# A recurrent-memory attention kernel: another order in its first segment, and output rows in one transfer

## The chip, the cores and the metric

The kernel runs on one core of a Trainium2 chip. The metric is the device time of one execution in microseconds (us), taken as the median of several runs. The engines are named as in the profile: PE (TensorE matmul) and PEld (its weight load), DVE (VectorE), ACT (ScalarE), POOL (GpSimd) and SP (SyncE). SP and POOL issue nearly all DMA transfers here; SP's go to the queue named q1 in the profile, POOL's to q0, and all of them run on the core's 16 DMA engines.

## What is computed

Two branches are mixed by a gate, on 2048 rows of 1024 values in bfloat16:

```python
g = sigmoid((x * gate_w).sum(-1, keepdims=True))
b = (gelu(x @ w_gate) * (x @ w_up)) @ w_down          # 1024 -> 3584 -> 1024
mem = mem0                                            # 8 rows
for s in range(64):                                   # segments of 32 rows
    h = concat([mem, x[32*s : 32*s+32]])              # 40 rows
    q, k, v = h @ Wq, h @ Wk, h @ Wv                  # 32 heads of 128
    p = softmax(where(mask, q @ k.T / sqrt(128), -1e9))
    o = (p @ v) @ Wo                                  # 40 rows of 1024
    mem = o[:8]
    a[32*s : 32*s+32] = o[8:]
out = g * a + (1 - g) * b
```

The mask lets every row see the 8 memory rows, and otherwise is causal. The attention branch is a recurrence: a segment needs the memory that the one before it produced. Its weights (4 x 8 MB) don't fit into SBUF.

## The kernel before

The program is written out by hand, instruction by instruction. A small scheduler (`_Sched`) takes each operation with its engine and the keys that it reads and writes, and puts in the semaphore waits. Each engine runs its operations in the order in which the program emits them, so the order of the `emit_` calls is the order of work on each engine, and POOL's and SP's transfers are issued in that order too. An operation that waits holds up all that stands behind it on its engine.

**Feed-forward branch (0 to about 597 us).** Four blocks of 512 rows: gate and up products, then the down product (L494). The last block's results go through SBUF buffers (`extra`, part of `arena`, `qk` and `oe`) and by 20 transfers on POOL's queue (L518) to DRAM, as `b_scr`. So `qk` can be overwritten only when its transfers have landed. In this time the attention weights begin to be loaded.

**Attention (597 us to the end): 64 segments.** A part of the weights stays in `arena`. The rest is streamed in every segment: 18 loads of 512 KB and one of 256 KB from a packed copy `w_scr` into `ring`, a buffer of 10 slots of 256 KB (L616, on SP). A load is issued when PE has freed its slots (`slot_free`). The main steps of a segment, with the names that the change touches:

- `emit_P(m, h, pos)`: one 1024-long product for m in q, k, v and half h of the heads, in eight pieces over the inner dimension (L948). `KORD` gives the order of the pieces for segments above 0, and `KCS` for segment 0. Pieces 6 and 7 come from the ring; in segment 0, pieces 4 and 5 of q/0 as well.
- In segment 0 each `emit_P` also does a product with `xe` (`emit_ext`, L835), which gives the first 8 rows of 4 segments ahead. Its result is copied to a staging area (`stage`, keys `rx` 0 to 4 in `arena` chunk 20, and `rowsx` for v/1) by ACT (L849). For q and k, PE then transposes it, DVE puts it back in another order (L874, 0.88 us) and POOL stores it as `qk_scr` (L877). The transposes and the rest form a job; `first_go` and `flush` emit the waiting jobs. For v, POOL stores it as `v_scr` (L852).
- `emit_T` (L992, L997, L999): transposes of q or k into `qk`. `emit_qke` (L1006): copies the extra rows from the staging area into `qk`.
- `emit_S(o)`: scores of pair o (L1025) and the softmax: DVE L1032 to L1036, Exp on ACT L1038, DVE L1039 to L1045, the last into `pn`. `emit_PT(o)`: transposes of `pn` (L1055) and a copy by DVE into `ptb` (L1060). `emit_PV(o)`: product with v (L1066) and copies by ACT into `oT` (L1074) and `oe` (L1075).
- `emit_vt` copies v to `vt` on ACT (L985). In segment 0 the extra rows of v come for half 0 by small transfers (`load_vte`, L720), and for half 1 by `emit_sel(par)`: a product with a selection matrix (L1195) and a copy by ACT (L1197).
- `emit_O(o, pos)`: product of the 8 heads of group o with Wo (L1107). In segment 0 `OHS` gives the order of the heads. Wo of heads 24 to 27 (group 3) lies in chunk 20, where the staging area was: `load_o3(k, xs)` (L885, on POOL) loads one of these four blocks over the staging places xs, and so waits for all that reads them.
- `keep`, `back`, `back_all`: pieces 4 and 5 of q/0 are kept in PSUM through the segment by transposes (L895, with a DVE copy at L901), and put back into free buffers at its end.

**The end of a segment.** ACT copies the 8 memory rows out (L1306), PE transposes them (L1317), DVE puts them into `hT` (L1322), and the next segment can start. DVE computes the gated mix into `bo` (L1325), a tile of 128 partitions by 256: partition 32*q + r holds columns 256*q to 256*q + 255 of row r. Four transfers on POOL's queue, one for each q, write it to the output (L1332), each with its own semaphore. Later in the next segment `load_b` loads `bo` again, when they have landed. In every fourth segment four more transfers (L1343) write the first 8 rows of four segments from `pn`, behind those of `bo` on POOL.

Of the kernel before, what the change touches and what calls it, by code (L numbers as in the profile page):

```python
# [128 lines left out]
def bass_gated_mix__memory_aug_recurrent_mem_tr__geglu_ffn__prompt_kernel(  # L129
# [38 lines left out]
    with ExitStack() as es:  # L168
# [367 lines left out]
                dst = chunk(c).rearrange("p (h d) -> p h d", h=4)  # L536
            op("sp", lambda e: e.dma_start(dst, src), w=[A(c)], dsem=f"a{c}")

        KCS = {0: (0, 6, 1, 2, 7, 3, 4, 5), ('k', 1): (6, 7, 0, 1, 2, 3, 4, 5), ('v', 1): (6, 7, 0, 1, 2, 3, 4, 5), ('v', 0): (6, 7, 0, 1, 2, 3, 4, 5), ('q', 1): (6, 7, 0, 1, 2, 3, 4, 5)}
        OHS = (0, 1, 4, 5, 2, 3, 6, 7)  # L540
        KORD = {('q', 0): (5, 6, 2, 1, 7, 3, 4, 0), ('q', 1): (0, 6, 1, 4, 7, 3, 5, 2), ('k', 0): (5, 2, 6, 7, 0, 1, 4, 3), ('k', 1): (0, 2, 3, 6, 7, 5, 4, 1), ('v', 0): (0, 6, 1, 2, 4, 3, 7, 5), ('v', 1): (4, 6, 1, 2, 7, 3, 0, 5)}
        OORD = ((1, 4, 5, 0, 2, 3, 6, 7), (0, 4, 1, 5, 3, 6, 2, 7), (0, 4, 1, 5, 2, 3, 6, 7), (0, 4, 1, 5, 2, 3, 6, 7))
# [185 lines left out]
        def rows_of(s):  # L728
            n = SEG if s + 1 < NSEG else NR
            v = of[s * SEG + EXT:s * SEG + EXT + n, :]  # L730
            return [(v[:, q * 256:(q + 1) * 256], bo[32 * q:32 * q + n, :]) for q in range(4)]
# [66 lines left out]
        for s in range(NSEG):  # L798
# [19 lines left out]
            def flush():  # L818
                while post:
                    go, put = post.pop(0)  # L820
                    put(go())


            def first_go():
                go, put = post.pop(0)
                put(go())
# [57 lines left out]
            def load_o3(k, xs):  # L884
                op("pool", lambda e: e.dma_start(chunk(20)[:, k * 1024:(k + 1) * 1024], A_Wo[24 + k, :, :]),  # L885
                   w=[("A20", k)] + [("rx", x) for x in xs], dsem=("b1", "b2", "b3", "a20")[k])
# [96 lines left out]
            def emit_vt(h, par, s=s):  # L983
                bank = acc(s, ("v", h))
                op("act", lambda e: e.activation(vt[0:2 * SEG, par, :], PB[bank][64 * par:64 * par + 64, :], ACTF.Copy),  # L985
                   r=[P(bank)], w=[("vt", par)])
# [11 lines left out]
                else:  # L998
                    op("dve", lambda e: e.tensor_copy(qk[:, m, :, 0:SEG, :], src), r=[P(B_T)], w=[("qk", m)])  # L999

            def emit_qke(h, s=s):
                if s == 0:
                    for mi, m in enumerate("qk"):
                        rx, kx, _ = stage(m, h)
                        src = rx[:, 0:128].rearrange("p (g x) -> p g x", g=4)
                        op("dve", lambda e, mi=mi, src=src: e.tensor_copy(  # L1006
                            qk[:, mi, :, SEG:L, :].rearrange("p g c i -> p g (c i)"), src), r=kx, w=[("qke",)])
                    if h == 1:
                        load_ext(1, 0)
                    return  # L1010
                op("dve", lambda e: e.tensor_copy(qk[:, :, :, SEG:L, :].rearrange("p m g c i -> p m g (c i)"), qkst[:, :, :, :]),
                   r=[("qkst",)], w=[("qke",)])
                if h == 1 and s + 1 < NSEG:
                    load_ext(s + 1, 0)
                elif h == 0:
                    load_ext(s, 1)
# [81 lines left out]

            def emit_O(o, pos, s=s, B_O=B_O):
                for x in pos:  # L1100
                    k = OORD[o][x] if s else OHS[x]
                    u, keys = unit(s, "o", o, k)

                    def mk(e, u=u, k=k, x=x):
                        ins = None
                        for q in range(4):
                            ins = e.matmul(PB[B_O][32 * q:32 * q + 32, 0:256], lhsT=oT[:, o % 2, k, :],  # L1107
                                           rhs=u[q // 2][:, (q % 2) * 256:(q % 2 + 1) * 256],
                                           start=(o == 0 and x == 0), stop=(o == NO - 1 and x == 7),
                                           skip_group_check=True)  # L1110
                        return ins
                    op("pe", mk, r=[("oT", o % 2)] + keys, w=[P(B_O)])
                    if "o" in jobs:
                        if k >= 4 and ("o", o, k) not in single:
                            do_oe(o, k, u, keys)
                        else:
                            later.append(lambda u=u, keys=keys, k=k: do_oe(o, k, u, keys))
                    slot_free(uses(s, "o", o, k))
# [11 lines left out]
                           r=[("bscr", jobs["o"], y) for y in range(GR)], w=[("rowsx", q)], dsem="be%d" % q)  # L1130

            if s == 0:
                emit_P("q", 0, ALL[:5])
                op("pe", lambda e: e.matmul(PB[B_S][:, 0:320], lhsT=pnz[:, 0:128], rhs=pnz, start=True, stop=True),
                   r=[("init", "pn")], w=[P(B_S)])
                emit_P("q", 0, ALL[5:])
                emit_P("k", 0, ALL[:5])
                emit_T(0)
                emit_P("k", 0, ALL[5:])
                emit_P("q", 1, ALL[:2])  # L1140
                first_go()
                sel = bo[:, 0:4 * EXT]
                op("dve", lambda e, sel=sel: e.tensor_copy(
# [3 lines left out]
                load_o3(3, (6,))  # L1147
                load_single(("o", 3, 4))
                load_single(("o", 3, 5))
                emit_P("q", 1, ALL[2:5])  # L1150
                emit_T(1)
                emit_P("q", 1, ALL[5:])
                emit_P("v", 0, (0,))
                first_go()
                emit_P("v", 0, ALL[1:6])
                first_go()
                emit_P("v", 0, (6, 7))
                emit_qke(0)
                emit_S(0)
                emit_vt(0, 0)  # L1160
                emit_vt(0, 1)
                load_vte(0, 0, 0)
                load_vte(0, 0, 1)
                vput.pop(0)()
                emit_P("k", 1, (0, 1, 2, 3, 4))
                emit_PT(0)
                emit_S(1)
                emit_T(0, "act")
                flush()
                emit_P("k", 1, (5, 6, 7))  # L1170
                emit_P("v", 1, (0, 1, 2))
                emit_T(1)
                emit_PV(0)
                emit_P("v", 1, (3,))
                emit_PT(1)
                emit_P("v", 1, (4,))
                flush()
                emit_qke(1)
                emit_P("v", 1, (5,))
                load_o3(2, (4,))  # L1180
                emit_PV(1)
                emit_P("v", 1, (6,))
                emit_S(2)
                emit_P("v", 1, (7,))
                load_x(1)
                load_o3(0, (0, 1))
                load_o3(1, (2, 3))
                emit_vt(1, 0)
                emit_vt(1, 1)
# [8 lines left out]
                       r=[P(bank)], w=[("vte", par), ("vte", par, 0)])  # L1198

                emit_O(0, ALL)  # L1200
                emit_O(1, LO)
                emit_sel(0)
                emit_O(1, (4, 5, 6))
                emit_PT(2)
                emit_S(3)
                emit_sel(1)
                load_b(0)
                emit_O(1, (7,))
                emit_PV(2)
                back_all("act", ("q", 0, 5, 1))  # L1210
                emit_O(2, ALL)
                emit_PT(3)
                emit_PV(3)
                back_all("dve", ("q", 0, 5, 0))
                emit_O(3, ALL)
# [112 lines left out]
            for put, bank in ends:  # L1328
                put(bank)
            last = s == NSEG - 1  # L1330
            for x, (d, b) in enumerate(rows_of(s)):
                op(("sp", "act")[x % 2] if last else "pool", lambda e, d=d, b=b: e.dma_start(d, b),  # L1332
                   r=[("bo", x)], w=[("out", s, x)], dsem="%s%d" % ("end" if last else "out", x))
            if "o" in jobs:
                j = jobs["o"]
                op("dve", lambda e, j=j: e.scalar_tensor_tensor(
# [52 lines left out]
```

## Time and profile before

| | us |
|---|---|
| median of 3 runs (lowest, highest) | 2498.48 (2494.85, 2501.15) |
| profiled execution, device time | 2490.87 |
| its span, first to last instruction | 2489.0 |
| PE busy | 2256.3 (91%) |
| DVE busy | 1169.8 (47%) |
| ACT busy | 930.9 (37%) |
| POOL busy | 653.4 (26%) |
| end of segment 0 (L1322 begins) | 646.0 |
| mean granted TensorE clock | 0.988 |

A busy PE in this profile is not PE at its peak, since matmuls are pipelined and their ends are modelled. POOL's busy time here is the time of building its DMA transfers. In a line of a group, the part after the bar is busy time and the mean of one instruction in ns, and then the idle time of the engine just before them with what ended it. In the timeline, the brackets hold the idle time before an instruction and what ended it. In a line of waits, the three numbers are the sum in us, how often, and the longest.

### The profile page before, as it was taken

To read this page: it belongs to the slowest core of one execution; us is meant where nothing else is said; L and a number is where in the kernel's file an instruction comes from. 1 tells how busy PE (TensorE), PEld (TensorE's weight loads), DVE (VectorE), ACT (ScalarE), POOL (GpSimd) and SP (SyncE) were. 2 spreads that over 40 slices of the span, in tenths; PEclk is the share of its full clock that TensorE was granted. 3 is DMA by queue.
4 is the path that set the end of the run, shared out by engine and by line. 5 is a ranking of instruction groups with operands and counts; after the bars stand their busy time and mean duration, and the time that the engine had idled before them with its cause. 6 is when DMAs were issued, how large, how long until landed. Compare 5 with 4: busy or idle time off the path is not lost.

```text
span 2489.0 us, 77539 instructions
## 1 busy us (share of the span) xinstructions
PE 2256.3 (91%) x33977; PEld 1112.8 (45%) x33977; DVE 1169.8 (47%) x3435; ACT 930.9 (37%) x2196; POOL 653.4 (26%) x1162
## 2 busy tenths in 40 slices
PE   9999999999889888988988898888889888889887
PEld 4444444444444444444444444444444444444443
DVE  5626264451444444544454544444444444455444
ACT  4314132221334343434443444434444434444433
POOL 1010103102232323233323323332323232323222
PEclk9999999999899999999999999999999999999988
DMA  8727354468999999999999999999999999999997
GB/s 273 257 71 256 97 179 123 144 229 302 322 348 365 365 371 348 373 359 379 375 377 354 374 366 374 352 356 367 375 370 378 365 363 376 362 377 374 371 362 281
DMA packets 328689, 797.10 MB, mean 320 GB/s; under 512 B 52728, under 2 KB 116456, under 8 KB 327584
## 3 DMA queue, kind: packets, MB, share of 16 engines
q1 hardware_dynamic: 284336, 736.78, 81.2%
q0 software_dynamic: 43872, 55.31, 7.1%
q8 instruction: 267, 4.37, 0.7%
q14 instruction: 70, 0.57, 0.1%
q10 hardware_dynamic: 144, 0.06, 0.0%
HBM read 764.52 MB, written 37.22 MB: 322 GB/s over the span
## 4 chain that ended last, share of the span: by engine, by line
PE 58%; DMA 26%; DVE 9%; ACT 4%; issue 3%; POOL 0%; SPq 0%; DVEq 0%; POOLq 0%
DMA ring<-w_scr 25%; PE pba L948 7%; PE pbb L948 7%; PE pbc L835 5%; PE pbb L1107 3%; PE pbe L1055 3%; PE pba L1107 2%; PE pbe L992 2%; PE pba L449 2%; PE pbb L449 2%; PE pbh L449 2%; PE pbg L449 2%; PE pbf L449 2%; PE pbe L449 2%; PE pbd L449 2%
## 5 line engine op out<-in xcount | busy, mean ns | idle before, releaser
L948 PE MATMUL pba<-arena,hT 128*32 128x512 bf16 x4416 | 350.6, 384 | 0.0
L948 PE MATMUL pbb<-arena,hT 128*32 128x512 bf16 x4416 | 342.6, 385 | 0.3 <-issue 0.3
L999 DVE COPY qk<-pbe 128x512 bf16<-128x512 bf16 x129 | 89.2, 692 | 363.3 <-PE pbe L992 358.6
L723 POOL DMA_DIRECT2D vt<-v_scr x252 | 147.9, 591 | 371.6 <-PE pbf L1066 234.1
L1038 ACT ACTIVATE pbd<-pbd 104x160 f32<-104x160 f32 x256 | 71.9, 281 | 432.2 <-DVE pbd L1036 432.2
L1060 DVE COPY ptb<-pbe 80x320 bf16<-80x320 bf16 x256 | 82.1, 321 | 240.5 <-PE pbe L1055 240.5
L1332 POOL DMA_DIRECT2D out_dram<-bo x252 | 125.8, 506 | 246.1 <-DVE bo L1325 244.9
L948 PE MATMUL pba<-ring,hT 128*32 128x512 bf16 x1542 | 153.2, 388 | 28.9 <-DMA ring<-w_scr 27.7
L835 PE MATMUL pbc<-arena,xe 128*32 128x512 bf16 x2208 | 174.4, 380 | 0.7 <-ACT rowsx L849 0.5
L948 PE MATMUL pbb<-ring,hT 128*32 128x512 bf16 x1536 | 151.9, 390 | 25.3 <-DMA ring<-w_scr 23.5
L954 ACT ACTIVATE rows<-pba 128x512 bf16<-128x512 f32 x128 | 76.6, 598 | 234.2 <-PE pba L948 234.2
L948 PEld LDWEIGHTS pba<-arena,hT 128*32 128x32 bf16 x4416 | 111.8, 97 | 97.9 <-issue 5.6
L1045 DVE TENSOR_TENSOR pn<-pbd,rr 104x256 bf16<-104x256 f32 (+1 forms) x512 | 142.3, 319 | 27.7 <-DMA out_dram<-pn 19.4
L948 PEld LDWEIGHTS pbb<-arena,hT 128*32 128x32 bf16 x4416 | 109.7, 97 | 93.0 <-issue 8.0
L954 ACT ACTIVATE rows<-pbb 128x512 bf16<-128x512 f32 x128 | 76.6, 598 | 173.7 <-PE pbb L948 173.6
L877 POOL DMA_DIRECT2D qk_scr<-rowsx x60 | 47.5, 791 | 344.2 <-DVE rowsx L874 281.6
L1107 PE MATMUL pba<-arena,oT 128*32 128x256 bf16 x2176 | 120.9, 281 | 14.1 <-ACT oT L1074 12.5
L1107 PE MATMUL pbb<-arena,oT 128*32 128x256 bf16 x2176 | 121.9, 279 | 12.7 <-ACT oT L1074 10.8
L1055 PE MATMUL pbe<-ident,pn 104*80 104x104 bf16 x1024 | 95.4, 216 | 40.9 <-DVE pn L1045 21.6
L1107 PE MATMUL pba<-ring,oT 128*32 128x256 bf16 x1792 | 107.0, 277 | 20.0 <-DMA ring<-w_scr 19.1
L1039 DVE TENSOR_REDUCE rs<-pbd 104x4 f32<-104x160 f32 x256 | 83.0, 324 | 88.9 <-ACT pbd L1038 88.9
L1107 PE MATMUL pbb<-ring,oT 128*32 128x256 bf16 x1792 | 113.5, 275 | 7.9 <-DMA ring<-w_scr 7.2
(260 smaller groups left out, 4355.2 us busy)
## 6 DMA issues: line engine op xcount, KB each, us to landing
ring<-w_scr SPq DMA_DIRECT2D x973, 512.0 KB, 6.3
ring<-w_scr SPq DMA_DIRECT2D x486, 256.0 KB, 5.9
arena<-in_B_w_gate_dram SPq DMA_DIRECT2D x27, 1024.0 KB, 5.5
arena<-in_B_w_up_dram SPq DMA_DIRECT2D x27, 1024.0 KB, 7.7
qkst<-qk_scr POOLq DMA_DIRECT2D x126, 64.0 KB, 5.2
qk_scr<-rowsx POOLq DMA_DIRECT2D x60, 128.0 KB, 5.6
arena<-in_B_w_down_dram SPq DMA_DIRECT2D x7, 1024.0 KB, 11.9
arena<-in_A_Wk_dram SPq DMA_DIRECT2D x6, 1024.0 KB, 6.9
```

The costliest lines, as they stand in the source:

```text
L449: ins = e.matmul(PB[bank][:, :], lhsT=wv[:, kc, col:col + 128], rhs=xb[:, kc, :], start=(kc == 0), stop=(kc == KC - 1))
L723: op("pool", lambda e: e.dma_start(vt[2 * SEG:KEYS, par, :], v_scr[s // GR, h, 2 * par:2 * par + 2, s % GR, :, :]), r=[("vscr", s // GR, h ...
L835: ins = e.matmul(PB[B_X][32 * gq:32 * gq + 32, :], lhsT=xe[:, us[-1], :], rhs=us[gq // 2][0][gq % 2], start=(n == 0), stop=(n == KC - 1), ...
L948: ins = e.matmul(PB[bank][32 * gq:32 * gq + 32, :], lhsT=hT[:, kc, :], rhs=us[gq // 2][0][gq % 2], start=(x == 0), stop=(x == KC - 1), ski ...
L954: op("act", lambda e: e.activation(rows[:, :], PB[bank][:, :], ACTF.Copy), r=[P(bank)], w=[("rows",)])
L999: op("dve", lambda e: e.tensor_copy(qk[:, m, :, 0:SEG, :], src), r=[P(B_T)], w=[("qk", m)])
L1039: op("dve", lambda e: e.tensor_reduce(rsv, sv, AX.X, ALU.add), r=[P(B_S)], w=[("rs",)])
L1045: op("dve", lambda e, c0=c0, k0=k0, n=n: e.tensor_tensor(out=pn[0:104, :, c0:c0 + 2 * n].rearrange("p i (two c) -> p i two c", two=2), in0 ...
L1055: ins = e.transpose(PBV[B_PT][0:KEYS, 512 + i * 128:512 + i * 128 + 104], pn[0:104, i, :], ident[0:104, 0:104])
L1060: op("dve", lambda e: e.tensor_copy(ptb[0:KEYS, :, :, :], src), r=[P(B_PT)], w=[("ptb",)] + first)
L1107: ins = e.matmul(PB[B_O][32 * q:32 * q + 32, 0:256], lhsT=oT[:, o % 2, k, :], rhs=u[q // 2][:, (q % 2) * 256:(q % 2 + 1) * 256], start=(o ...
L1332: op(("sp", "act")[x % 2] if last else "pool", lambda e, d=d, b=b: e.dma_start(d, b), r=[("bo", x)], w=[("out", s, x)], dsem="%s%d" % ("en ...
```

## The change

Two things are changed. In segment 0 the order of many steps is another one: q/0 takes its pieces in another order, `emit_S(0)` and its copies come ahead of most of v/0, `emit_qke(1)` is split into its q and its k copy, Wo blocks 0 and 2 are loaded earlier, the flush of k/1's job and `emit_PV(0)` change places with pieces of v/1, the selection products stand elsewhere, and group 3 of the output product takes its heads in another order. In all segments but the last, the four output transfers are one, which has the four column blocks as its outer dimension on the DRAM side and all 128 partitions on the SBUF side, with one semaphore.

```diff
-        KCS = {0: (0, 6, 1, 2, 7, 3, 4, 5), ..., ('q', 1): (6, 7, 0, 1, 2, 3, 4, 5)}
+        KCS = {0: (0, 6, 1, 2, 7, 3, 4, 5), ..., ('q', 1): (6, 7, 0, 1, 2, 3, 4, 5), ('q', 0): (0, 6, 7, 4, 5, 1, 2, 3)}
+        OHS3 = (3, 4, 5, 6, 7, 2, 0, 1)
         OHS = (0, 1, 4, 5, 2, 3, 6, 7)
...
-            def emit_qke(h, s=s):
+            def emit_qke(h, s=s, ms=(0, 1)):
                 if s == 0:
-                    for mi, m in enumerate("qk"):
+                    for mi in ms:
+                        m = "qk"[mi]
...
-                    if h == 1:
+                    if h == 1 and ms[-1] == 1:
                         load_ext(1, 0)
...
-                    k = OORD[o][x] if s else OHS[x]
+                    k = OORD[o][x] if s else (OHS, OHS, OHS, OHS3)[o][x]
...
             if s == 0:
-                emit_P("q", 0, ALL[:5])
+                emit_P("q", 0, (0,))
                 op("pe", lambda e: e.matmul(PB[B_S][:, 0:320], lhsT=pnz[:, 0:128], rhs=pnz, start=True, stop=True),
                    r=[("init", "pn")], w=[P(B_S)])
-                emit_P("q", 0, ALL[5:])
+                emit_P("q", 0, (1, 2, 3, 4, 5, 6, 7))
                 emit_P("k", 0, ALL[:5])
                 emit_T(0)
                 emit_P("k", 0, ALL[5:])
-                emit_P("q", 1, ALL[:2])
+                emit_P("q", 1, ALL[:3])
                 first_go()
...
-                emit_P("q", 1, ALL[2:5])
+                emit_P("q", 1, ALL[3:5])
                 emit_T(1)
                 emit_P("q", 1, ALL[5:])
-                emit_P("v", 0, (0,))
                 first_go()
-                emit_P("v", 0, ALL[1:6])
-                first_go()
-                emit_P("v", 0, (6, 7))
+                emit_P("v", 0, (0, 1, 2))
                 emit_qke(0)
                 emit_S(0)
+                emit_P("v", 0, (3, 4))
+                first_go()
+                emit_P("v", 0, (5, 6, 7))
                 emit_vt(0, 0)
                 emit_vt(0, 1)
                 load_vte(0, 0, 0)
                 load_vte(0, 0, 1)
                 vput.pop(0)()
-                emit_P("k", 1, (0, 1, 2, 3, 4))
+                emit_P("k", 1, (0, 1, 2, 3))
                 emit_PT(0)
                 emit_S(1)
+                emit_qke(1, ms=(0,))
+                load_o3(0, (0, 1))
+                load_o3(2, (4,))
                 emit_T(0, "act")
-                flush()
-                emit_P("k", 1, (5, 6, 7))
+                emit_P("k", 1, (4, 5, 6, 7))
                 emit_P("v", 1, (0, 1, 2))
                 emit_T(1)
+                emit_P("v", 1, (3,))
+                flush()
+                emit_P("v", 1, (4,))
                 emit_PV(0)
-                emit_P("v", 1, (3,))
                 emit_PT(1)
-                emit_P("v", 1, (4,))
-                flush()
-                emit_qke(1)
+                emit_qke(1, ms=(1,))
                 emit_P("v", 1, (5,))
-                load_o3(2, (4,))
+                emit_S(2)
                 emit_PV(1)
-                emit_P("v", 1, (6,))
-                emit_S(2)
-                emit_P("v", 1, (7,))
+                emit_P("v", 1, (6, 7))
                 load_x(1)
-                load_o3(0, (0, 1))
                 load_o3(1, (2, 3))
...
                 emit_O(0, ALL)
+                emit_sel(0)
                 emit_O(1, LO)
-                emit_sel(0)
-                emit_O(1, (4, 5, 6))
                 emit_PT(2)
                 emit_S(3)
+                emit_O(1, HI)
+                emit_PV(2)
                 emit_sel(1)
                 load_b(0)
-                emit_O(1, (7,))
-                emit_PV(2)
-                back_all("act", ("q", 0, 5, 1))
                 emit_O(2, ALL)
                 emit_PT(3)
+                back_all("act", ("q", 0, 5, 1))
                 emit_PV(3)
                 back_all("dve", ("q", 0, 5, 0))
                 emit_O(3, ALL)
...
             last = s == NSEG - 1
-            for x, (d, b) in enumerate(rows_of(s)):
-                op(("sp", "act")[x % 2] if last else "pool", lambda e, d=d, b=b: e.dma_start(d, b),
-                   r=[("bo", x)], w=[("out", s, x)], dsem="%s%d" % ("end" if last else "out", x))
+            if last:
+                for x, (d, b) in enumerate(rows_of(s)):
+                    op(("sp", "act")[x % 2], lambda e, d=d, b=b: e.dma_start(d, b),
+                       r=[("bo", x)], w=[("out", s, x)], dsem="end%d" % x)
+            else:
+                op("pool", lambda e, s=s: e.dma_start(
+                    of[s * SEG + EXT:(s + 1) * SEG + EXT, :].rearrange("r (q c) -> q r c", q=4), bo[:, :]),
+                   r=[("bo", x) for x in range(4)], w=[("out", s, x) for x in range(4)], dsem="out0")
```

More of the change, by code (lines that the diff above doesn't have):

```diff
@@ L537, in load_need @@
             op("sp", lambda e: e.dma_start(dst, src), w=[A(c)], dsem=f"a{c}")
-        KCS = {0: (0, 6, 1, 2, 7, 3, 4, 5), ('k', 1): (6, 7, 0, 1, 2, 3, 4, 5), ('v', 1): (6, 7, 0, 1, 2, 3, 4, 5), ('v', 0): (6, 7, 0, 1, 2, 3, 4, 5), ('q', 1): (6, 7, 0, 1, 2, 3, 4, 5)}
+        KCS = {0: (0, 6, 1, 2, 7, 3, 4, 5), ('k', 1): (6, 7, 0, 1, 2, 3, 4, 5), ('v', 1): (6, 7, 0, 1, 2, 3, 4, 5), ('v', 0): (6, 7, 0, 1, 2, 3, 4, 5), ('q', 1): (6, 7, 0, 1, 2, 3, 4, 5), ('q', 0): (0, 6, 7, 4, 5, 1, 2, 3)}
+        OHS3 = (3, 4, 5, 6, 7, 2, 0, 1)
         OHS = (0, 1, 4, 5, 2, 3, 6, 7)
```

## The prediction

> **What bounds the kernel now.** I read the page's slices first, then its queues and its chain, then windows around the first segment and over the rest, then the two places that the change edits: the first segment's instructions in order of time, and POOL's groups. From the page:
>
> ```profile
> PEclk9999999999899999999999999999999999999988
> DMA  8727354468999999999999999999999999999997
> ...
> q1 hardware_dynamic: 284336, 736.78, 81.2%
> q0 software_dynamic: 43872, 55.31, 7.1%
> ...
> PE 58%; DMA 26%; DVE 9%; ACT 4%; issue 3%; POOL 0%; SPq 0%; DVEq 0%; POOLq 0%
> ```
>
> From slice 11 on, the DMA engines are busy without a gap. The chain names weight loads (26%) and PE, no POOL: the ring that SP feeds and the PE that empties it release one another. One engine moves 736.78 MB / (0.812 x 16 x 2489 us) = 22.8 GB/s. Windows of the whole core (us, then PE, PEld, DVE, ACT, POOL busy, PEclk, DMA share, GB/s):
>
> ```profile
> 625.00:630.00 5.00, 4.69 (x80) 2.26 (x76) 2.47 (x9) 2.27 (x6) 0.00 (x0) 1.00 0.56 203
> 630.00:635.00 5.00, 4.74 (x113) 2.91 (x106) 3.54 (x15) 2.79 (x7) 2.91 (x5) 1.00 0.80 243
> 635.00:640.00 5.00, 2.83 (x47) 1.36 (x45) 2.26 (x9) 2.44 (x6) 2.14 (x4) 0.79 0.92 331
> 640.00:645.00 5.00, 2.56 (x38) 1.30 (x36) 1.01 (x2) 0.50 (x2) 0.00 (x0) 0.50 1.03 411
> ...
> 700.00:2389.00 1689.00, 1495.49 (x28292) 757.94 (x28290) 808.27 (x2750) 690.64 (x1659) 521.10 (x917) 1.00 1.00 367
> ```
>
> Segments 1 to 63 are DMA-bound (share 1.00), so an edit there is worth what it changes in DMA work. Segment 0 (597 to 646 us) is not: PE loses 4.6 us in 635 to 645, and DMA loses 3.2 us in 625 to 635. The end of segment 0, in order of time:
>
> ```profile
> 635.89 0.54 POOL L885 DMA_DIRECT2D arena<-in_A_Wo_dram  x1 [1.89 <-DMA qk_scr<-arena]
> ...
> 636.45 0.59 ACT L1197 ACTIVATE vt<-pbb 16x512 bf16<-16x512 f32 x1
> ...
> 637.06 0.38 ACT L1074 ACTIVATE oT<-pbf 128x256 bf16<-128x256 f32 x1
> ...
> 637.50 0.40 PE L1107 MATMUL pba<-arena,oT 128*32 128x256 bf16 x8 [1.82 <-ACT oT L1074]
> ...
> 643.41 0.62 PE L1107 MATMUL pba<-arena,oT 128*32 128x256 bf16 x8 [1.55 <-DMA arena<-in_A_Wo_dram]
> ```
>
> Two stalls stand out: 1.82 us for oT of pair 2, whose copy queues on ACT behind the second selection's copy (0.59), and 1.55 us for a Wo block whose load left POOL at 635.89 and landed 7.5 us later.
>
> **Segment 0, part by part.** (a) q/0 takes pieces 7, 4, 5 earlier and the dummy matmul moves up. The transposes of 4 and 5 now end inside q/0; they cost PE two stalls of 0.46 (604.29, 606.14). I count 0: the chain has b_scr<-qk from 605.45 for 5.27 us, and the first copy into qk (L999) can't begin before it lands (610.85), so PE waits there anyway. Without that cover it would be -0.9.
>
> (b) S(0) moves ahead of v/0's last five pieces. Before, PE lost 0.33 at S(0) and 0.55 at PT(0). After, S(0) follows three pieces (3 x 0.22) behind k/0's transposes, but needs the staging copy (0.88) and two copies (0.42): about 0.9 lost; the softmax (2.7 us) then runs beside v/0, and PT(0) loses nothing. Sum 0, between -0.9 and +1.1.
>
> (c) POOL's queue. q/1's staging store now stands behind that softmax on DVE, so it leaves about 1.5 us later than 620.26, and the four vt<-arena loads (2.1 us) with it; PV(0) is moved back by two pieces and a flush, which hides that; uncovered it costs 1.5. Wo blocks 0 and 2 are issued early, but block 2 overwrites v/0's stage and waits for v_scr, issued near 625 and 5.2 us to landing: POOL stands until 630. Behind it stand k/1's store, qkst, hT and Wo block 1. So k/1's store leaves at about 630.5 (before 631.09), and block 1, which waits for that store (4.5 us), lands about 0.6 earlier, near 642.8. Splitting qke(1) moves two copies of 0.21 and hides in DVE's idle time.
>
> (d) sel(1) after PV(2) takes its 0.59 off ACT ahead of oT: -0.6. S(3)'s Exp stays ahead of oT, so the other 1.2 remain. sel(0) now follows only O(0); it may lose up to 0.4 to ACT.
>
> (e) O(3) in order 3, 4, 5, 6, 7, 2, 0, 1 uses block 1 last. Before, the last 7 heads ran after 643.41 at half clock (to 645.1); after, one runs past 642.8: -1.4, between -1.9 and 0. back_all("act") behind PT(3) has 1.03 us of ACT time while O(2) runs: 0.
>
> Sum -2.0, between -4.7 and +3. It survives, since DMA's idle time in 610 to 660 exceeds it.
>
> **The output transfer, 63 times.** POOL's groups, by form:
>
> ```profile
> L1332 POOL DMA_DIRECT2D out_dram<-bo x244 | 121.8, 506 | 233.7 <-DVE bo L1325 232.5 <-issue 1.2
> ...
> L1343 POOL DMA_DIRECT2D out_dram<-pn x60 | 35.5, 599 | 0.1
> ...
> L737 POOL DMA_DIRECT2D bo<-b_scr x60 | 33.1, 552 | 3.3 <-issue 2.1 <-DMA out_dram<-bo 0.6
> ```
>
> Four issues of 506 ns become one of 552 (128 rows, L737) to 599 (four blocks, L1343): -1.4 us of POOL per segment, off the path (POOL is busy 31%). The wait is the same as before, on one DVE instruction, so nothing new queues behind it.
>
> In DMA work, the trace's packet records after 600 us have POOL's completions as 4 B packets of 9.4 ns: 48 fewer over 16 engines, -28 ns. The old transfers show as 16 packets of 1,024 B (46.6 ns) each. The 16 KB transfers of L1343, four blocks on the DRAM side, show none of that size: they go in 4 packets of 4,096 B (177 ns), with twelve fillers of 32 B (14.3 ns). The new transfer has four blocks too, so I take 16 packets of 4,096 B on four engines: 16 x 177 against 64 x 46.6 is -9 ns per engine, the fillers +11. Sum -26 ns, x 63 = -1.7 us. The other side: four engines get 16 KB where each had 4, 0.72 against 0.18 us, and every ring load waits for its slowest engine: +0.54 us x 63 = +34. I take no loss: by the issues and landings of the ring, three or more loads (1.4 us each at 367 GB/s) are under way 93% of the time, so an engine 0.54 behind doesn't leave the others idle, if the four engines change from segment to segment. That they do is likely: vt<-v_scr has two blocks, and 32 KB per segment always on the same two would hold them 1.4 us of 29, leaving DMA at 0.95, not 1.00.
>
> The page "DMA: Bandwidth & Descriptors" of the Trainium skill (section "Why a DMA increments its semaphore by 16 and not by 1") lets a transfer use the largest k up to 16 that divides the slowest dimension of both sides, and lets GpSimd's transfers rotate over the engines. Its k of 4 here agrees with the four packets above; the rotation no row shows directly. By the section "Rules for kernel authors" of the same page of the Trainium skill, four small transfers should be one large one, which would promise a gain where the k rule threatens a loss.
>
> Every fourth segment, POOL's output rows stand ahead of the four stores of pn; these would leave 1.4 us sooner.
>
> ```profile
> DVE pn L1045 <- DMA out_dram<-pn: 19.4, 13, 2.6
> ```
>
> I take 0: in these segments the transposes that need pn begin 1.3 to 2.7 us after pn is written. The bound is what DMA idles there: by the packets its share is 0.978 of 28.6 us, so 15 x 0.63 = -9.
>
> **Sum.** -2.0 - 1.7 = -3.7 us. The profiled execution took 2490.87 us (span 2489.0 and 1.9 around it), 0.3% under the median of the runs shown, 2498.48 (2494.85 to 2501.15). So 2487.2 for a profiled one and 2494.8 for the median. Within 0.3% (7.5 us, about what a measurement of this kernel can tell from no change).
>
> **Rivals.** R1, slower: the four loaded engines set the pace. The landing of a ring load slips by up to 0.54 us, and PE frees its slot later. It decides from 0.18 us per segment (11.2 us against the -3.7); at half the lag, +17 - 3.7 gives 2512. For it: the chain alternates between ring and PE; against it: the depth of the ring. With the same four engines each time it would be all +34, 2529. (The Trainium skill's rotation, cited above, speaks against this last case.) R2, faster: the pn stores were on the path: -9 - 3.7 gives 2486. Against it stands the gap before the transposes. R3, faster: segment 0 gives back more: both stalls whole (-3.4), the transposes' 0.9, and 2.5 us of PE work that 637.9 to 645 ran at 0.50 clock done before it: -6.8 - 1.7, 2490. R4, slower: POOL's stand at Wo block 2 makes hT and block 1 late; by 12 us, which no row nears: 2507.
>
> **How the numbers follow.** Forecast 0.38, R1 0.22, R2 0.20, R3 0.14, R4 0.06. So faster 0.34, same 0.38, slower 0.28. The forecast's own range is 2491 (the lower bound of its case) to 2503 (segment 0 at +3, the transfer at -1.7, and 3 us that the shown runs spread about their median). For 8 in 10 I go to 2483 (R2 and R3 with the runs' spread of 3) and to 2512 (R1 at half lag).
>
> **What would show it.** L1332's successor once per segment at 0.55 to 0.60 us, with 16 packets of 4,096 B; ring waits on PE no larger than before (R1: larger in all segments, DMA share under 0.99); segments 700 to 2389 at 367 GB/s. In segment 0: one late Wo head instead of seven, oT's stall near 1.2, mem's copy (L1322) near 644 instead of 646.0. The pn wait near 5 us with DMA's share in those segments still 0.98; at 1.00, R2. If segment 0 ends after 646, (b) or (c) was undersized.

## The result, and the profile after

The changed kernel took 2502.78 us (median; 2494.65 to 2508.67), the kernel before, on the same chip, 2494.85 (2487.29 to 2504.08). The ratio is 1.0031, with a 95% interval of 1.0018 to 1.0044: slower by about 7.7 us, where 3.7 us of gain was forecast. The profiled execution has a span of 2503.3 us. Its page, the lines that answer to those shown of before (slices of the span, then the two queues' packets, MB and share, then the chain by engine):

```profile
PEclk9999999999999999999999999999999999999989
DMA  8727254468999999999999999999999999999998
...
q1 hardware_dynamic: 284336, 736.78, 81.1%
q0 software_dynamic: 40848, 55.40, 7.1%
...
PE 56%; DMA 29%; DVE 8%; ACT 3%; issue 2%; POOL 0%; SPq 0%; DVEq 0%; POOLq 0%
```

The queue that SP feeds moved the same packets. POOL's queue moved 3,024 packets fewer, 48 a segment. The chain has 3 points more of DMA and 2 fewer of PE. The windows (length, then busy us of PE, PEld, DVE, ACT, POOL, then PEclk, DMA share, GB/s):

```profile
625.00:630.00 5.00, 4.45 (x80) 2.08 (x72) 2.08 (x9) 1.40 (x4) 0.60 (x2) 1.00 0.84 289
630.00:635.00 5.00, 4.73 (x115) 3.02 (x108) 3.25 (x13) 3.01 (x9) 2.36 (x4) 1.00 0.91 317
635.00:640.00 5.00, 2.24 (x45) 1.27 (x45) 2.06 (x8) 2.39 (x5) 2.13 (x4) 1.00 1.01 344
640.00:645.00 5.00, 2.80 (x46) 1.30 (x47) 1.28 (x3) 2.14 (x6) 0.00 (x0) 0.61 1.02 403
700.00:2389.00 1689.00, 1481.38 (x28000) 749.77 (x28000) 796.06 (x2708) 681.69 (x1636) 443.20 (x739) 0.99 1.00 363
```

The first four lines are segment 0. DMA's share rose there from 0.56 to 0.84 and from 0.80 to 0.91: the loads that came early filled idle time, as meant. The last line is where the time went in this profile. At an unchanged DMA share of 1.00 the rest of the kernel ran at 363 GB/s instead of 367. By the starts of successive segments, one took 29.41 us on average where it had taken 29.12. The two profiled executions lie 14.3 us apart, about twice the 7.7 of the medians, so a pair of profiles overstates the loss. The extra shows in PE's waits for the ring (the page's groups; the last part of a line is idle time ahead of the group, and what ended it):

```profile
L949 PE MATMUL pba<-ring,hT 128*32 128x512 bf16 x1542 | 153.6, 389 | 34.1 <-DMA ring<-w_scr 33.1
L949 PE MATMUL pbb<-ring,hT 128*32 128x512 bf16 x1536 | 150.7, 387 | 35.1 <-DMA ring<-w_scr 33.7
```

Before, these two groups (then at L948) waited 27.7 and 23.5 us for the ring. The sum is 15.6 us more. But such sums move by up to 20 us from one profile to the next (below), so the verdicts rest on the ratios.

**Segment 0** in order of time (start, busy of one, engine, line, instruction, and in brackets the idle time before it and what ended it):

```profile
617.36 0.34 PE L1027 MATMUL pbd<-qk 128*40 128x40 bf16 x8 [0.55 <-DVE qk L1008]
...
621.67 0.76 POOL L878 DMA_DIRECT2D qk_scr<-arena  x1 [3.47 <-DVE arena L875]
...
630.45 0.54 POOL L886 DMA_DIRECT2D arena<-in_A_Wo_dram  x1 [3.88 <-DMA v_scr<-arena]
...
630.98 0.77 POOL L878 DMA_DIRECT2D qk_scr<-arena  x1
...
636.21 0.54 POOL L886 DMA_DIRECT2D arena<-in_A_Wo_dram  x1 [3.40 <-DMA qk_scr<-arena]
636.33 0.40 PE L1109 MATMUL pba<-arena,oT 128*32 128x256 bf16 x8 [0.77 <-ACT oT L1076]
...
638.65 0.40 PE L1109 MATMUL pba<-ring,oT 128*32 128x256 bf16 x8 [1.49 <-DMA ring<-w_scr]
...
642.86 0.40 PE L1109 MATMUL pba<-arena,oT 128*32 128x256 bf16 x4 [0.95 <-DMA arena<-in_A_Wo_dram]
...
644.19 0.19 DVE L1322 COPY hT<-pbe 128x64 bf16<-128x64 bf16 x1 [3.29 <-PE pbe L1317]
```

mem's copy, the last line, stood at 646.02 before: in this pair of profiles segment 0 ends 1.8 us sooner, and PE waits for Wo block 1 with one head (four matmuls) left instead of seven. **The output transfer** and the wait that it touches (POOL's groups, and DVE's wait, from 700 us on):

```profile
L1336 POOL DMA_DIRECT2D out_dram<-bo x61 | 44.7, 732 | 233.6 <-DVE bo L1325 221.9 <-issue 11.7
```

```profile
DVE pn L1047 <- DMA out_dram<-pn: 1.9, 4, 0.9
```

One issue of 732 ns replaces four of 506, so POOL is free 1.3 us sooner in each segment. The wait for pn's stores fell from 19.4 us to 1.9.

### The profile page after: what moved, and what is told of

It is laid out like the page before. It is cut to its first block, busy times and chain, and to the rows that moved or that the text cites. A ratio compares the mean times of both kernels' runs of the same rounds, so it can differ in the third digit from the quotient of the medians.

```text
span 2503.3 us, 77171 instructions
## 1 busy us (share of the span) xinstructions
PE 2250.6 (90%) x33921; PEld 1111.4 (44%) x33977; DVE 1168.8 (47%) x3435; ACT 931.4 (37%) x2196; POOL 571.1 (23%) x973
## 4 chain that ended last, share of the span: by engine, by line
PE 56%; DMA 29%; DVE 8%; ACT 3%; issue 2%; POOL 0%; SPq 0%; DVEq 0%; POOLq 0%
DMA ring<-w_scr 28%; PE pba L949 7%; PE pbb L949 6%; PE pbc L836 4%; PE pbb L1109 3%; PE pbe L1057 2%; PE pbe L993 2%; PE pba L1109 2%; PE pba L449 2%; PE pbb L449 2%; PE pbg L449 2%; PE pbd L449 2%; PE pbc L449 2%; PE pbh L449 2%; PE pbf L449 2%
## 5 line engine op out<-in xcount | busy, mean ns | idle before, releaser
L878 POOL DMA_DIRECT2D qk_scr<-rowsx x60 | 47.2, 787 | 361.8 <-DVE rowsx L875 295.7
L712 POOL DMA_DIRECT2D qkst<-qk_scr x126 | 70.4, 559 | 230.5 <-DVE qk L1013 229.4
```

## The experiments

Ratios are to the kernel before on the same chip in the same set of runs, with 95% intervals. The theory behind the first set: the loss sits in the output transfer, either because its 64 KB lie on four DMA engines (R1; the expectations call it T1), or because its single issue lets POOL's next transfers leave sooner (T2). A third theory, T3, puts it into the new order of segment 0.

**Each part alone.** The new segment 0 with the four old transfers:

```diff
-KCS = {0: (...), ...}
+KCS = {0: (...), ..., ('q', 0): (0, 6, 7, 4, 5, 1, 2, 3)}
+OHS3 = (3, 4, 5, 6, 7, 2, 0, 1)
...
-                emit_P("q", 0, ALL[:5])
+                emit_P("q", 0, (0,))
...
```

> The other part of the change alone: the new order of segment 0, with the four output transfers of the kernel before. T1 and T2 (the cause lies in the output transfer): -1.8 us, ratio 0.9993, segment 0 ending near 644.2 us. T3 (phase of segment 0): the loss is here, +8, ratio 1.003.

It measured 0.9993 (0.9970 to 1.0017). Its segment 0 ends at 644.27. So the loss doesn't come from there. The other half, the old segment 0 with one transfer of four blocks:

```diff
-for x, (d, b) in enumerate(rows_of(s)):
-    op(... "pool", lambda e, d=d, b=b: e.dma_start(d, b), ...)
+op("pool", lambda e, s=s: e.dma_start(
+    of[s * SEG + EXT:(s + 1) * SEG + EXT, :].rearrange("r (q c) -> q r c", q=4), bo[:, :]), ..., dsem="out0")
```

> The kernel before with one part of the change: a segment's output rows leave in one transfer with four column blocks as its outer dimension; segment 0 is as before. Three theories of the 7.8 us that the changed kernel lost. T1 (few engines): 64 KB go through four of the 16 DMA engines, 16 KB each, and the ring's loads wait for these four; the changed kernel gained about 1.8 us in segment 0, so T1 expects the loss whole: +9.5 us, ratio 1.0038, and PE's waits for the ring up as in the changed kernel. T2 (early POOL): the single issue frees POOL 1.3 us sooner in each segment, and the small transfers behind it collide with the ring: also +9.5. T3 (phase): the new order of segment 0 sets the ring off in a worse phase: 0 here, ratio 1.000.

It measured 1.0048 (1.0022 to 1.0074). The transfer loses by itself, 12 us by this ratio.

**The number of blocks.** The same 64 KB in one transfer, with the slowest dimension on the DRAM side cut into 16 blocks, or into two (the rows then land in another order inside the segment):

```diff
+of[...].rearrange("r (q c) -> (r q) c", q=4).rearrange("(b a) c -> a b c", a=16), bo[:, :]
+of[...].rearrange("r (q c) -> (r q) c", q=4).rearrange("(b a) c -> a b c", a=2), bo[:, :]
```

> The kernel before, with the output rows of a segment in one transfer too, but its outer dimension on the DRAM side is 16 blocks of 8 strips of 512 B instead of 4 blocks of 32. The strips land in another order inside the same 64 KB, so the output's rows are permuted; bytes, strips and the one issue on POOL are the same. T1 (few engines): 4 KB on each of 16 engines, as the four old transfers had: between -3 and 0 us, ratio 0.999 to 1.000. T2 (early POOL): the same loss as with 4 blocks, +9.5. T3 (phase of segment 0): 0.

> As the run with 16 blocks, but with 2 blocks of 64 strips: again one transfer of 64 KB per segment with one issue, output rows permuted inside the segment. T1 (few engines): two engines carry 32 KB each, 1.44 us at 22.8 GB/s instead of 0.18 on every engine, so the lag is 1.26 us per segment against 0.54 with 4 blocks: about 2.3 times the loss, +22 us, ratio 1.009. T2 (early POOL): +9.5 as with 4 blocks. T3 (phase): 0.

Sixteen blocks measured 1.0024 (1.0001 to 1.0047), two blocks 1.0121 (1.0090 to 1.0152). Two blocks lie above four with the intervals apart; 16 and four are not told apart, and even 16 seems to lose a little. The issue's price follows the blocks as well. The groups of the transfer in three kernels, 16 blocks, four and two:

```profile
L1336 POOL DMA_DIRECT2D out_dram<-bo x58 | 32.1, 554 | 202.7 <-DVE bo L1325 193.5 <-DVE pn L1340 9.2
```

```profile
L1336 POOL DMA_DIRECT2D out_dram<-bo x58 | 42.5, 734 | 194.0 <-DVE bo L1325 194.0
```

```profile
L1336 POOL DMA_DIRECT2D out_dram<-bo x57 | 47.9, 840 | 196.3 <-DVE bo L1325 186.0 <-DVE pn L1340 10.3
```

The window of the two-block kernel:

```profile
700.00:2389.00 1689.00, 1472.85 (x27698) 743.59 (x27690) 791.06 (x2693) 676.61 (x1623) 444.69 (x729) 0.99 0.99 360
```

It looks like the changed kernel's, further along: 360 GB/s. With 32 KB on two engines R1's lag is 2 x 0.72 - 0.18 = 1.26 us a segment; the loss of 30.2 us is 0.48 a segment, 0.38 of it. Part of it is DMA work: by the packet records POOL's queue sends 112 packets of 32 B a segment more than before, 15.2 ns each. Over 16 engines that is 106 ns, and with what the one transfer saves some 5 us over the kernel, an estimate.

To see if a descriptor pattern was at fault, the 64 KB went as 128 contiguous strips (`rearrange("r (q c) -> (r q) c", q=4)` alone):

> The kernel before with a segment's output rows in one transfer of 128 strips of 512 B that lie one behind another in DRAM (rows permuted inside the segment), so 16 blocks or more on both sides. It repeats the run with 16 blocks, which was 0.24% slower with an interval from 0.01% to 0.47%, with another order of the strips. T1 (few engines) alone: -3 to 0 us, ratio 0.999 to 1.000. If a part of the loss comes from the early POOL issue (T2) or from 64 KB leaving in one burst: +4 to +8 us, ratio 1.002 to 1.003, as there.

It measured 1.0019 (1.0002 to 1.0037), as with 16 blocks: no difference between the two orders of the strips shows, and a small loss stays.

**Smaller lumps elsewhere.** If lumps on few engines hold the ring back, the two-block vt loads of the kernel before should do so too. Each was split into two loads of one block of eight rows:

```diff
-op("pool", lambda e: e.dma_start(vt[2 * SEG:KEYS, par, :], v_scr[s // GR, h, 2 * par:2 * par + 2, s % GR, :, :]), ...)
+for side in range(2):
+    g0, p0 = 2 * par + side, 2 * SEG + EXT * side
+    op("pool", lambda e, g0=g0, p0=p0: e.dma_start(vt[p0:p0 + EXT, par, :], v_scr[s // GR, h, g0, s % GR, :, :]), ...)
```

> The kernel before, output transfers as they were; instead each of the four vt loads of a segment (16 KB, two blocks of 8 rows of 1 KB) becomes two loads of 8 rows. T1 (few engines), with the share of the lag that the runs so far let through (12 us of 34 with 4 blocks, about 0.36): a vt load puts 8 KB on each of two engines, 0.36 us at 22.8 GB/s, and afterwards 1 KB on each of eight, so eight engines in a segment lose a lag of 0.32 us; 0.36 x 0.32 x 63 = 7 us less, and 64 more completions of 9.4 ns on 16 engines give 2.4 us back: about -5 us, ratio 0.998, between -10 and +3. If lumps of 8 KB are too small to reach PE: 0 to +3. A theory in which POOL's issues matter (T2) expects a change too, since POOL is busy about 2 us more in each segment: slower by some us.

It measured 1.0035 (1.0012 to 1.0057), a loss where a gain was expected. PE's waits name a new one, which the kernel before doesn't have:

```profile
PE pbf L1068 <- DMA vt<-v_scr: 6.6, 9, 1.2
```

Four more issues a segment make POOL later, and vt now comes late. The run says little about lumps; it was the first sign that a later POOL costs.

**Another engine issues.** The four old transfers, and the one of four blocks, leave from ACT's queue, so that POOL's timing is the same in both (POOL's first load behind it starts 0.51 us after the transfer's start by the median, where the changed kernel has 0.74):

```diff
-op(("sp", "act")[x % 2] if last else "pool", lambda e, d=d, b=b: e.dma_start(d, b), ...)
+op(("sp", "act")[x % 2] if last else "act", lambda e, d=d, b=b: e.dma_start(d, b), ...)
```

> The kernel before with its four output transfers issued by ACT instead of POOL, from that queue's own descriptors; the control of the next run. Each has 32 rows, so it should lie on 16 engines. Both theories: near the kernel before, between -5 and +10 us (ACT spends four issues, 312 to 617 ns as in the last segment before, 1.3 to 1.9 us in each segment, where it is busy 37%).

> One output transfer per segment with four blocks, issued by ACT. T1 (few engines): if ACT's transfers always take the same four engines, as the Trainium skill's page DMA: Bandwidth & Descriptors (section Why a DMA increments its semaphore by 16 and not by 1) has it for this queue (the lowest-numbered k), nothing lets these engines catch up: 12 KB more on each in every segment, 0.54 us x 63 = +34 us against the control with four transfers, ratio 1.0136. If they rotate, or if only the momentary lag counts: +10 to +13, as on POOL. T2 (early POOL): equal to the control.

Four transfers measured 1.0019 (0.9998 to 1.0040), one of four blocks 1.0029 (1.0009 to 1.0048): a difference of 2 us, not told from none. Were the same four engines loaded each time and at their limit, it would be R1's 34. Nor is the control told from the kernel before, though POOL is free even earlier in it than in the changed kernel. So no cost of an early POOL by itself shows here, though up to 10 us would fit the interval. The semaphore of the merged transfer goes up in five steps, those of the four old ones in 16 each. (By the Trainium skill, "DMA: Bandwidth & Descriptors", section "Why a DMA increments its semaphore by 16 and not by 1", a transfer from such a queue spreads over the largest k up to 16 that divides the slowest dimension on both sides, and its semaphore jumps by 16 - k at once and then rises by 1 for each engine; the five steps agree with a k of 4.)

**POOL's timing.** The second theory: what costs is that POOL's later issues start 1.3 us sooner. In the trace only the first issues behind the output transfer do so (medians of the starts, 700 to 2389 us, counted from the transfer's own start). The first of two loads, nearly always of vt, moves from 1.99 to 0.74 us; the load or store behind these two waits for other engines and stays near 7 us (7.27 and 6.67). In every fourth segment the stores of pn stand ahead of the two loads. First a kernel that differs from the one before by a comment alone:

```diff
-    NEG = -1.0e9
+    NEG = -1.0e9  # unchanged
```

> The kernel before, with one comment changed and no instruction. Kernels with quite different edits lay 0.19% to 0.48% above the kernel before, some of them against expectation, so this run asks what the comparison itself gives. T1 (few engines) and T2 (early POOL): 0 us, ratio 1.000 within 0.2%. If it lies at 1.002 like the others, a part of their losses is no effect of their edits.

It measured 0.9998 (0.9976 to 1.0020), so the loss isn't one of the comparison. Then four memsets on POOL of 0.366 us each, 1.46 us in all, behind the transfer, which put the first load back to 2.33 us behind the four-block transfer's start, 2.14 behind the 16-block one's. Nothing reads the partitions of ptb that they fill:

```diff
+if not last:
+    for _ in range(4):
+        op("pool", lambda e: e.memset(ptb[96:128, :, :, :], 0.0))
```

The same four lines went behind the 16-block transfer, the four-block one, and the four old transfers:

> The run with one transfer of 16 blocks, and behind each transfer's issue four memsets of a free corner of ptb (partitions 96 to 127, 320 columns, an estimated 0.37 us each by the memset of pn, 128x320), so that POOL reaches the issues behind it 2.0 us after the start, as with four transfers. T2 (early POOL makes the 0.2% of the runs with 16 blocks): back to the kernel before, between -3 and +2 us. T1 alone has no room for a change: as without the memsets, +5 (ratio 1.002).

> The run with one transfer of 4 blocks (the change's own) and the same four memsets on POOL behind each issue. T1 (a burst of 16 KB on each of four engines, which delays the ring's loads for a moment): the loss stays, +7 to +12 us, ratio 1.003 to 1.005. T2 (early POOL alone): back to 0. Both together: about +6, half of the loss without memsets.

> The kernel before with its four output transfers, and the four memsets behind them: POOL reaches the next issues 1.5 us later than before, with no transfer changed. T2 in a narrow form (earlier is worse): 0 or a small gain, -3 to 0. T2 in a wide form (the order of the segments fits this timing of POOL, and every other timing loses): +3 to +8. T1: 0.

The 16-block kernel measured 1.0015 (0.9993 to 1.0038), the four-block one 1.0008 (0.9986 to 1.0029), and the old transfers, whose followers now start 3.58 us behind them, 1.0029 (1.0008 to 1.0050). Doing nothing but delay costs; adding work to the merged kernel costs nothing, and may win. What the delay costs the old kernel can be read in its waits, first as in the kernel with the comment, then with the memsets:

```profile
DVE pn L1045 <- DMA out_dram<-pn: 23.4, 13, 3.7
PE pbe L1055 <- DVE pn L1045: 21.0, 50, 0.7
```

```profile
DVE pn L1045 <- DMA out_dram<-pn: 43.2, 15, 4.3
PE pbe L1055 <- DVE pn L1045: 31.0, 58, 3.5
```

The stores of pn leave later, DVE waits for them 20 us more, and PE 10 us more for DVE; the loss is 7 us by the ratio. So a late POOL has a path of its own that can carry the loss, and this run says nothing about an early one. Group and window of the four-block kernel with its memsets, and the window of the same kernel without them:

```profile
L1341 POOL MEMSET ptb<- 32x320 bf16 x232 | 85.0, 366 | 10.0
```

```profile
700.00:2389.00 1689.00, 1493.93 (x28288) 757.15 (x28280) 807.69 (x2749) 689.37 (x1658) 527.89 (x975) 1.00 1.00 367
700.00:2389.00 1689.00, 1492.37 (x28228) 755.82 (x28228) 806.10 (x2742) 688.24 (x1654) 447.05 (x743) 1.00 1.00 367
```

With memsets POOL is as busy as before (528 against 521 us). The rate doesn't tell the two apart: the profile without memsets was taken in that kernel's fastest execution (2489.90 us) and has 367 GB/s too. By the ratios, four blocks with and without memsets stood at 1.0008 and 1.0048 with intervals that overlap. So the pair was taken again, with the two-block one and, above all, the changed kernel itself with the memsets:

> The changed kernel whole (new order of segment 0, one transfer of four blocks), with the four memsets on POOL behind each output transfer, which give the issues behind it the timing of the kernel before. T2 (POOL's timing): the loss goes, and segment 0's gain is left: -2 us, ratio 0.999 to 1.000. T1 (lump): still slower by 5 to 9 us, ratio 1.002 to 1.0035.

> The same kernel as the run with one transfer of four blocks and the old segment 0, which lay at 1.0048 (1.0022 to 1.0074); repeated beside the next run on one chip. Both theories: 1.003 to 1.005. If it lies at 1.001 or below, the first value was too high by chance and the comparison with the memsets says little.

> The same kernel as the run with one transfer of four blocks and four memsets, which lay at 1.0008 (0.9986 to 1.0029). T2: 1.000 to 1.001 again, and at least 0.2% under the run without memsets. T1: equal to that run, 1.003 to 1.005.

> One transfer of two blocks (32 KB on each of two engines; rows permuted inside the segment), which lay at 1.0121 without memsets, now with the four memsets behind it. T1: the loss is the lump's and stays, 1.009 to 1.012. T2: most of it goes, 1.000 to 1.004. Both together (a lump that large and the transfers close behind it): about half, 1.005 to 1.008.

The table holds all of these, by what follows the transfer on POOL:

| output rows of a segment | nothing added | 1.46 us of memsets behind |
|---|---|---|
| four transfers (before) | 0.9998 (0.9976 to 1.0020; the comment) | 1.0029 (1.0008 to 1.0050) |
| one, 16 blocks | 1.0024 (1.0001 to 1.0047) | 1.0015 (0.9993 to 1.0038) |
| one, 4 blocks | 1.0048 (1.0022 to 1.0074) | 1.0008 (0.9986 to 1.0029) |
| the same again | 1.0035 (1.0011 to 1.0059) | 1.0019 (0.9994 to 1.0044) |
| one, 2 blocks | 1.0121 (1.0090 to 1.0152) | 1.0073 (1.0048 to 1.0098) |
| the changed kernel | 1.0031 (1.0018 to 1.0044) | 0.9995 (0.9973 to 1.0017) |

Two things are read from it. Down the right column, with POOL's timing about as it was, two blocks still lose 18 us and four lose little. That is more than the 5 us of added DMA work, so a lump on two engines costs by itself. Across the rows, 1.46 us of useless work on POOL gives back 9 us in the changed kernel, where the intervals just part (1.0018 against 1.0017), 12 with two blocks, where they touch (1.0090 against 1.0098), and 10 and 4 with four blocks, where they overlap. The repeat fell short of the 0.2% that T2 had named. All four have the same sign, but with 16 blocks nothing is told apart (1.0024 and 1.0019 without memsets, 1.0015 with), though POOL is as early there. So the memsets help behind a lump; that an early POOL costs without one is not shown.

**Where on POOL.** What the delay works on could be the own time of the loads behind the transfer, or their distance from it. The memsets stood ahead of the four-block transfer (the first load again 0.75 us behind its start), or eight of them behind it (4.01 us):

```diff
+if not last:
+    for _ in range(4):
+        op("pool", lambda e: e.memset(ptb[96:128, :, :, :], 0.0), r=[("bo", 0)])
+op("pool", lambda e, s=s: e.dma_start(of[...].rearrange("r (q c) -> q r c", q=4), bo[:, :]), ...)
```

```diff
+op("pool", lambda e, s=s: e.dma_start(of[...].rearrange("r (q c) -> q r c", q=4), bo[:, :]), ...)
+if not last:
+    for _ in range(8):
+        op("pool", lambda e: e.memset(ptb[96:128, :, :, :], 0.0))
```

> One transfer of four blocks with the old segment 0, and the four memsets of 0.37 us ahead of it on POOL (they wait for the same DVE instruction), so that the transfer and what stands behind it both go out 1.5 us later, as close to one another as without memsets. Closeness: the loss stays, 1.003 to 1.005. Own time of the loads behind: the loss goes as with the memsets behind the transfer, 1.000 to 1.002.

> One transfer of four blocks with the old segment 0, and eight memsets behind it instead of four: the loads behind it start 3.0 us later than without, 1.7 us later than in the kernel before. Closeness: a wider gap is no worse, 1.000 to 1.002. Own time: as far past the time of the kernel before as the changed kernel is ahead of it, so a loss again, like four transfers with memsets (1.0029): 1.002 to 1.004.

They measured 1.0022 (0.9998 to 1.0046) and 1.0026 (1.0003 to 1.0049), between the four-block kernel with four memsets behind it and without any. With eight memsets the stores of pn are late again, as in the delayed old kernel: DVE waits 40.6 us for them and PE 28.1 for pn, where four memsets behind the transfer gave 17.3 and 20.5. That is 8 us of PE's time and may be all of this run's loss, so the run doesn't refute the distance. On what the delay works stays open.

## Why the prediction was wrong

**Segment 0: right in its steps, and its size by some luck.** The sum was -2.0 and the two profiles show -1.8 (646.02 to 644.19). Profiles of one and the same order differ by as much: from its first product (L948) to L1322 segment 0 took 47.2 to 49.0 us in the 17 profiles with the old order (mean 48.2), and 46.1 to 47.4 in the three with the new one (mean 46.8). So the gain is near 1.4 us, and the ratio of segment 0 alone (0.9993, 0.9970 to 1.0017) is too wide to tell it from none. The steps, in the pair of profiles:
- (b) S(0) lost 0.55 us where 0.9 was allowed for.
- (c) q/1's store left at 621.67 (forecast 1.5 behind 620.26, so 621.8). POOL stood at Wo block 2 until 630.45 (630), k/1's store followed at 630.98 (630.5), and block 1 was there at 642.86 (642.8).
- (d) oT's stall is 0.77 (1.2), and a head of O(2) now waits 1.49 for the ring, which no step named.
- (e) One late Wo head, as forecast, with a stall of 0.95. R3 (6.8 us of gain) and R4 (12 of loss) both fell with this.

**The output transfer: wrong.** The step that failed is "I take no loss": the term was -1.7 us and it measured about +9 (7.7 for the whole change, plus the 1.4 to 1.8 that segment 0 gave), and +12.0 and +8.7 for the transfer alone, so near 0.15 us a segment. Two sentences carried the step. "An engine 0.54 behind doesn't leave the others idle" holds for four engines within the noise only with POOL's timing restored (1.0008 and 1.0019), and for two engines not even then (1.0073). Its reason was the ring's depth, put at three loads or more for 93% of the time; from issue to landing it is even 99% of 700 to 2389 us, and the loss came all the same. And "-1.4 us of POOL per segment, off the path" took POOL's freed time as worth nothing in either direction. The runs show that behind a transfer of few blocks it is not: giving the time back with memsets gives the changed kernel's loss back. What moves in the trace is the two loads behind the transfer, mostly of vt, and every fourth time the stores of pn ahead of them. How their early start hurts is not shown. A lump and loads close behind it, both together, would suit the 16-block runs, which have no lump and lie at 1.0015 to 1.0024, but is only argued. ACT's merged transfer has the loads of POOL as close behind it, on another queue, and there the lump costs 2 us, not told from none.

**R1** had the sign, and the time falls into the range to which it reached. That 2502.78 also lies inside the forecast's own range, to 2503, is no merit: that end was reached by a segment 0 at +3, which didn't come. R1's mechanism is a part of the cause only. The loss is 0.28 of its full lag (0.15 of 0.54 us), most of it goes with POOL's timing, and its worst case, the same engines always at their limit, didn't come: 9 to 12 us from POOL and 2 from ACT, instead of 34.

**R2** fell. The wait for pn's stores went from 19.4 to 1.9 us, in the merged kernel to 5.5, and no gain showed. DMA's share in those segments did not rise: by the packets from one L1322 to the next it is 0.974 after 0.986, the prediction's count having 0.978. The 0 taken for it was right.

**Sizes.** The issue takes 732 ns, not 552 to 599: the nearest row, of the same number of blocks, carried a quarter of the bytes. The fillers came as 48 a transfer instead of 12, by the packet records (1,504 of 32 B in POOL's queue before, 4,528 after). At 14.3 ns each over 16 engines that is 43 ns a segment instead of 11, and turns the -26 ns of DMA work into about +6, which is 0.4 us over 63 segments, so it doesn't explain the loss.

**The signs that were named** worked unequally. The 16 packets of 4,096 B came (1,008 more over 63 segments), but they come with 16 blocks and with two as well, so they don't show the number of engines. 363 instead of 367 GB/s pointed at the loss, but the merged kernel alone, slower by its ratio, showed 367. The sum of PE's ring waits did not serve: in single profiles (L948 and L1107, or their successors, weight loads included) it was 218 us before, 221 with the comment, 240 with segment 0 alone (0.9993). For four blocks it was 236 without memsets and 219 with, and the other way round in the repeat, 218 and 234. Only two blocks stand out, at 260. And a DMA share of 1.00 stayed 1.00 through a loss of 0.3%.

No version was measurably faster than the kernel before. The changed kernel with memsets (0.9995) and segment 0 alone (0.9993) come nearest.

## What to carry to other kernels

When several transfers become one, count the blocks of its slowest dimension: few blocks put the bytes on few DMA engines, and at 64 KB two blocks cost here some 0.7 to 1.2%. Then ask what the freed time of the issuing engine sets in motion, for "off the path" is no price: here 1.46 us of useless work behind a transfer of few blocks gave back 4 to 12 us, and behind the four old transfers cost 7. A few idle instructions that restore the old timing tell that effect from the transfer's own. And take a second profile of an unchanged kernel before reading a difference of one or two us from a pair: here one order of segment 0 spread over 1.8 us.

## What the hardware showed that was not expected

- The issue of a 64 KB transfer on POOL gets dearer with fewer blocks: 554 ns for 16, 732 to 734 for four, 840 for two.
- POOL's output transfers of few blocks add packets of 32 B: 48 with four blocks, 112 with two, none with 16. The counts fit four on each of twelve engines and eight on each of 14, the ones left out. The same transfer from ACT's queue adds none. vt's loads of two blocks have 28 of 16 B, which fits two on each of 14.
- 16 KB on each of four engines in place of 4 KB, 63 times, made from ACT a difference of 2 us that isn't told from none, where a full lag would be 34. DMA's share of 700 to 2389 us was 0.99 or 1.00 in every kernel here, at 360 to 368 GB/s, so a share of 1.00 doesn't say that nothing can be lost or gained.
